# Two attentions mixed by a gate: x loaded with features first, and the gate's row sums taken by PE

## The chip, the cores and the metric

The kernel runs on one core of a Trainium2 chip. The metric is device time in microseconds, smaller is better. The engines are called as in the profile: PE (TensorE, products), PEld (its weight loads), DVE (VectorE), ACT (ScalarE), POOL (GpSimd) and SP (SyncE, which issues most DMAs). A line number such as L279 is a line of the kernel before.

## The reference, cut to what matters

```python
x = A_x                                          # 1 x 2048 x 512, float32
g = sigmoid((x * gate_w).sum(-1, keepdims=True)) # one gate per row of x
a = infini_attention(x, wq, wk, wv, wo, beta)    # 4 segments of 512 rows, causal, with a memory M, z
b = attention(x, wqkv, wo_b)                     # 32 heads of 16, all 2048 rows
return g * a + (1 - g) * b
```

In `infini_attention` each segment's rows also retrieve from the memory of the segments before: `a_mem = (phi(q) @ M) / (phi(q) @ z + 1e-6)`, which is mixed with the causal attention of the segment by `sigmoid(beta)` per head. Everything is float32.

## The kernel before, in words

**Precision.** A product of two float32 operands is made of three products of rounded operands: each operand is split into a rounded part (hi) and the rest (lo), and hi·hi, hi·lo and lo·hi are summed (TERMS). So x, with its 512 features on partitions, is kept twice, as xh (tile XH) and xl (tile XL); weights likewise (ws for q and k, wv for v).

**The x stage** (L642 to L679). x comes as 16 tiles of 128 rows, rows on partitions. SP loads a tile of 256 KB into one of 8 slots of the tile RAW (load_x, L159). PE transposes it in four 128x128 pieces into a PSUM bank (do_x, L168), ACT copies the bank to xh (L171), DVE subtracts to get xl (L172). The gate's row sums are taken on DVE from the same raw tile: dot_gate (L177) multiplies a tile by gate_w, which lies on all 128 partitions (tile gw, 256 KB of DMA), and accumulates along the row into a column of `gate`. After its dot a slot is free, and the loads of tiles 8 to 15 go there. Between these steps stand the eight jobs qk_job(0, "B", 0, w, c): q (w=0) and k (w=1) of the first eight heads of attention B, for each chunk c of 512 rows, 12 products each (L279). A job's result is copied by ACT and DVE into st, one of four buffers, and SP stores it to DRAM in two DMAs (L295). `for c in range(4)`: job w=0, then do_x of the four tiles of the next chunk, two dots and two loads, job w=1, two dots and two loads. POOL loads the weights (L234, L242); the first of them go to VA and to VB[0] (list `flat`), the later ones round the 8 slots of RAW (raw_buf).

**v of attention A** (L686 to L700). 16 jobs v_job("A", tt) of 12 products each (L262), copied by ACT into one of two buffers VS (both lie in VB[0]), stored by SP for two jobs at a time (L269). After job 2 come the split of A's q and k weights and do_gate (sigmoid of the 16 columns of `gate`), after job 3 SP's 12 small loads of beta (L182). POOL loads those weights, and then sends constant rows into the k and q tiles (set_aux, L148). PSUM banks are taken in turn, the one longest unused first (misc; six banks here).

**The 16 blocks** (L722 to L805). For each group of heads g and chunk c: q and k of A, memory out (mem_out, L304), transposes of phi(k) (mem_tr), the memory's output put back by rows (mem_put, L323), and one or more tasks of the list `fill` (v of B, q and k of B's other heads). mem_out writes the retrieved rows to the tile om, mem_put transposes om on PE, scales it back into om, and SP copies om to DRAM (L331). There is one om buffer, so the next block's mem_out waits until that DMA has read it. Near the end of the blocks SP also issues the loads of k for the attention loop (load_kb, L369) and the rows of maxima (m_rows, L484).

**The attention loop** (L905 to L939) runs 32 rounds over both attentions: products of k and q (t_group, L503), exp on ACT (L509), products with v (pv, L525), and ahead of them the products and maxima (s_b, L449 and L451) of the next round. Then come the tail and the output.

The order of each engine's work is the order of the calls in the program; nothing reorders them. A DMA on SP stands behind what was issued before it, and it is issued when what it waits for is done.

Of the kernel before, what the change touches and what calls it, by code (L numbers as in the profile page):

```python
# [7 lines left out]
FT = mybir.dt.float32  # L8
FR = mybir.dt.float32r
BF = mybir.dt.bfloat16  # L10
I32 = mybir.dt.int32
AF = mybir.ActivationFunctionType
OP = mybir.AluOpType
# [5 lines left out]
E = 16  # L19
SEQ = 2048  # L20
DM = 512
C = 512
NC4 = SEQ // C
NT = SEQ // 128
# [6 lines left out]


@with_exitstack
def gated_mix_kernel(ctx, tc, x, wq, wk, wv, wo, beta, wqkv, wob, gate_w, out):
    nc = tc.nc
    xr = x.rearrange("b s d -> (b s) d")
    outr = out.rearrange("b s d -> (b s) d")

    P = ctx.enter_context(tc.tile_pool(name="persist", bufs=1))
    W = ctx.enter_context(tc.tile_pool(name="work", bufs=2))  # L40
# [10 lines left out]
    ident = P.tile([128, 128], FT, name="ident")  # L51
    cmask = P.tile([128, 2, 128], BF, name="cmask")
    crows = P.tile([128, 2, 128], BF, name="crows")
    gate = P.tile([128, NT], FT, name="gate")
# [5 lines left out]
    RAW = P.tile([128, 8, C], FT, name="raw8")  # L60
    PTILE = [RAW[:, 4 * n:4 * n + 4] for n in range(2)]
    xh = [P.tile([128, 2, 4, C], FR, name=f"xh{n}") for n in range(2)]
    XH = [xh[c // 2][:, c % 2] for c in range(NC4)]
    flat = [VA[n].rearrange("p t h e -> p (t h e)")[:, :DM] for n in range(2)]
    vflat = VB[0].rearrange("p t h e -> p (t h e)")
    flat += [vflat[:, n * DM:(n + 1) * DM] for n in range(4)]
    RAWV = flat + [RAW[:, n] for n in range(8)]
    KB = [P.tile([128, 2, SEQ], FR, name="kb0")] + [t.rearrange("p a k t -> p a (k t)") for t in xh]

# [1 line left out]
    X = proj.enter_context(tc.tile_pool(name="proj", bufs=1))  # L71
    XL = [X.tile([128, 4, C], FR, name=f"xl{c}") for c in range(NC4)]
# [15 lines left out]
    def bank(allowed):  # L88
        b = min(allowed, key=lambda a: max([n for n, x in enumerate(lru) if x is a], default=-1))
        lru[:] = [x for x in lru if x is not b] + [b]  # L90
        return b
# [3 lines left out]
    def misc():  # L95
        return bank(mode["misc"])
# [17 lines left out]
    def raw_buf():  # L114
        i = cnt.get("raw", 0)
        cnt["raw"] = i + 1
        return RAWV[i if i < 6 else 6 + (i - 6) % 8]


    def identity():  # L120
        jp = X.tile([128, C], FT, name="phi0").bitcast(I32)[:, :128]
        nc.gpsimd.iota(jp, pattern=[[1, 128]], base=0, channel_multiplier=-1)
        nc.vector.tensor_scalar(ident, jp, 0.0, None, op0=OP.is_equal)

        for j in range(2):
            r = slice(64 * j, 64 * j + 64)
            for n in range(2):
                o = 64.0 * (n - j)
                nc.vector.tensor_scalar(crows[r, n], jp[r], o, None, op0=OP.is_equal)
                nc.vector.tensor_scalar(cmask[r, n], jp[r], o, MASK, op0=OP.is_gt, op1=OP.mult)  # L130
# [18 lines left out]
                                         aux[:, a, None, :].to_broadcast([E, n, 64]))  # L149


    gw = X.tile([128, DM], FT, name="gw")

    def load_gate():
        nc.sync.dma_start(gw, bass.AP(tensor=gate_w.tensor, offset=gate_w.offset, ap=[[0, 128], [1, DM]]))

    XR = {}

    def load_x(tt):  # L159
        XR[tt] = RAW[:, tt % 8]  # L160
        nc.sync.dma_start(XR[tt], xr[tt * 128:(tt + 1) * 128, :])

    def do_x(tt):
        c, tl = divmod(tt, 4)
        xt = XR.pop(tt)
        b = misc().rearrange("p (k t) -> p k t", k=4)
        for k in range(4):
            nc.tensor.transpose(b[:, k, :], xt[:, k * 128:(k + 1) * 128], ident)  # L168
        hi = XH[c][:, :, tl * 128:(tl + 1) * 128]
        lo = XL[c][:, :, tl * 128:(tl + 1) * 128]  # L170
        nc.scalar.activation(hi, b, AF.Copy)  # L171
        nc.vector.tensor_tensor(lo, b, hi, op=OP.subtract)  # L172
        XG[tt] = xt

    XG = {}

    def dot_gate(tt):  # L177
        scr = W.tile([128, DM], BF, name="scr", bufs=1)
        nc.vector.scalar_tensor_tensor(scr, XG.pop(tt), 1.0, gw, op0=OP.mult, op1=OP.mult,
                                       accum_out=gate[:, tt:tt + 1])  # L180

    def load_beta():  # L182
        for g in range(4):
# [13 lines left out]

    def do_gate():
        e = X.tile([128, NT], FT, name="ge")
        nc.scalar.activation(e, gate, AF.Exp, scale=-1.0)  # L200
        nc.vector.tensor_scalar(e, e, 1.0, None, op0=OP.add)
        nc.vector.reciprocal(gate, e)

# [16 lines left out]
    def split(hi, lo, raw):  # L220
        nc.scalar.activation(hi, raw, AF.Copy)
        nc.vector.tensor_tensor(lo, raw, hi, op=OP.subtract)

    def wcols(kd, w):
        if kd == "A":
            return (wq, wk, wv)[w], 0
        return wqkv, w * DM

    WR = {}

    def load_wv(kd, k):
        src, c0 = wcols(kd, 2)
        WR[k] = raw_buf()
        nc.gpsimd.dma_start(WR[k], src[k * 128:(k + 1) * 128, c0:c0 + DM])  # L234

    def split_wv(k):
        split(WV[0][:, k, :], WV[1][:, k, :], WR.pop(k))

    def load_w_raw(kd, g, w):
        src, c0 = wcols(kd, w)  # L240
        raw = raw_buf().rearrange("p (k c) -> p k c", k=4)
        nc.gpsimd.dma_start(raw, src.rearrange("(k p) c -> p k c", p=128)[:, :, c0 + g * 128:c0 + (g + 1) * 128])  # L242
        return raw

    def load_w(kd, g):
        WR[kd, g] = [load_w_raw(kd, g, w) for w in range(2)]

    def split_w(n, kd, g, ws=(0, 1)):
        for w in ws:
            split(WS[n][w][0], WS[n][w][1], WR[kd, g][w])  # L250
# [50 lines left out]
    def mem_state(g, c):  # L301
        return MST[c % 2][g % 2]

    def mem_out(g, c):  # L304
        m = mem_state(g, c)[:, :, :E + 1]
        o = X.tile([128, 4, 8, E], FT, name="om")
        r = X.tile([128, 4, 8], FT, name="recm")
        for n in range(2):
            b = misc()[:, :16 * (E + 1)].rearrange("p (i h e) -> p i h e", i=2, h=8)
            for i in range(2):  # L310
                nc.tensor.matmul(b[:, i], PHI[g, 0, c][:, (2 * n + i) * 128:(2 * n + i + 1) * 128], m,
                                 start=True, stop=True)
            nc.scalar.activation(r[:, 2 * n:2 * n + 2], b[:, :, :, E], AF.Copy)
            nc.scalar.activation(o[:, 2 * n:2 * n + 2].rearrange("p i h e -> p (i h) e"),
                                 b[:, :, :, :E].rearrange("p i h e -> p (i h) e"), AF.Copy)
        nc.vector.tensor_scalar(r, r, 1e-6, None, op0=OP.add)
        nc.vector.reciprocal(r, r)
        nc.vector.tensor_tensor(r, r, gate[:, 4 * c:4 * c + 4, None].to_broadcast([128, 4, 8]), op=OP.mult)
        o3 = o.rearrange("p i h e -> p (i h) e")
        nc.vector.tensor_tensor(o3, o3, r.rearrange("p i h -> p (i h)")[:, :, None].to_broadcast([128, 32, E]), op=OP.mult)  # L320
        PHI[g, "o", c] = o
# [19 lines left out]
    def load_vm(g, c):  # L341
        PHI[g, "v", c] = X.tile([128, 4, 8, E + 1], FT, name="vm", bufs=2)
        v_src(PHI[g, "v", c], "A", g, c)
# [45 lines left out]
    def load_kb(k, c=None):  # L389
        dst = KB[k % 3] if c is None else KB[k % 3][:, :, c * C:(c + 1) * C]  # L390
        load_qk(dst, "B", 1, k % 8, c)
# [247 lines left out]
    def s_tasks(u):  # L639
        return [todo(s_a, u, *t) for t in ST_A] if u < 32 else [todo(s_b, u, *t) for t in ST_B]  # L640

    for tt in range(4):  # L642
        load_x(tt)
    identity()
    load_w("B", 0)
    for tt in range(4, 8):
        load_x(tt)
    load_gate()
    constants()

    for tt in range(3):
        do_x(tt)
    split_w(0, "B", 0, (0,))
    do_x(3)
    split_w(0, "B", 0, (1,))
    def dots(tt):
        for t in (tt, tt + 1):
            dot_gate(t)
            if t + 8 < NT:
                load_x(t + 8)  # L660

    dots(0)
    dots(2)
    for c in range(NC4):
        for w in range(2):
            qk_job(0, "B", 0, w, c)
            if c + 1 < NC4:
                if w == 0:
                    for t in range(4):
                        do_x(4 * c + 4 + t)  # L670
                dots(4 * c + 4 + 2 * w)
            elif w == 0:
                split_wv(3)
        if c == 1:
            for k in range(4):
                load_wv("A", k)
        if c == 2:
            for k in range(3):
                split_wv(k)  # L679
# [6 lines left out]
    for tt in range(NT):  # L686
        v_job("A", tt)
        if tt == 2:
            split_w(0, "A", 0)
            do_gate()  # L690
        if tt == 3:
            load_beta()
        if tt in (7, 9, 11):
            load_wv("B", (tt - 7) // 2)
        if tt == NT - 1:
            load_vm(0, 0)
            load_kb(0)
            load_q(32)
        if ax:
            set_aux(*ax.pop(0))  # L700
# [21 lines left out]
    for blk in range(16):  # L722
        g, c = divmod(blk, 4)
# [9 lines left out]
        n = blk + 1 + (c == 2)  # L733
# [222 lines left out]
    for t in range(4):  # L956
        d = den[:, t * 128:(t + 1) * 128]
        o = o_cols(3, t)[:, 3, 0]
# [36 lines left out]
```

## Time and profile before

| | us |
|---|---|
| median of 3 runs | 1981.27 (1977.9 to 1982.19) |
| span of the profiled execution | 1976.0 |
| x stage: PE busy in the first 44 us | 35.19 |
| of it the transposes (L168) | 10.34 |
| the attention loop, from 350 us to the end | 1626 |

How to read the profile: a row of a group gives line, engine, operation, output<-input, shapes, count, then busy time and mean ns, then the idle time ahead of it and what ended it. A timeline row gives the start and the length in us, engine, line, and in brackets the idle time before it and its releaser. The chain of work that ended last gives the start and the length of each piece. The granted clock is that of PE, 1.00 at full speed. "SPq" is the time in which SP issues a DMA, or waits in doing so.

### The profile page before, as it was taken

How to read it: one execution, taken by the hardware profiler on the slowest of the kernel's cores; microseconds unless marked ns; L12 is line 12 of the kernel's file. 1: busy time of each engine (PE TensorE's matmuls, PEld its weight loads, DVE VectorE, ACT ScalarE, POOL GpSimd, SP SyncE). 2: the span in 40 equal slices, each digit the busy share in tenths (PEclk: the TensorE clock that was granted, in tenths of full speed). 3: DMA queues.
4: the chain of work that ended last, by engine and by line, in shares of the span. 5: the costliest groups of instructions: out<-in, count | busy, mean ns of one | idle time of the engine just before them, and what ended most of it. 6: DMA issues, size and time to landing. Idle time of an engine off the chain costs nothing.

```text
span 1976.0 us, 43643 instructions
## 1 busy us (share of the span) xinstructions
PE 1944.8 (98%) x17517; PEld 945.6 (48%) x17517; DVE 1630.3 (83%) x1825; ACT 1435.7 (73%) x2703; POOL 257.5 (13%) x474
## 2 busy tenths in 40 slices
PE   8999999999999999999999999999999999999999
PEld 6887777434344344444444444444444444444435
DVE  6135665899999999999999999999999999999942
ACT  3233332688888888888888888888888888888884
POOL 2200000011210101111010101010101010101012
PEclk9999999999999999999999999999999999999999
DMA  6766656644443444344445353444344444444111
GB/s 205 172 209 183 191 186 173 152 111 114 97 114 88 103 86 103 86 114 86 114 85 112 86 113 86 114 86 114 86 108 91 96 102 87 102 90 103 48 51 57
DMA packets 162742, 222.49 MB, mean 113 GB/s; under 512 B 39260, under 2 KB 89452, under 8 KB 156780
## 3 DMA queue, kind: packets, MB, share of 16 engines
q1 hardware_dynamic: 159596, 211.70, 44.0%
q0 software_dynamic: 2944, 8.00, 2.1%
q8 instruction: 138, 2.26, 0.5%
q14 instruction: 64, 0.52, 0.1%
HBM read 148.21 MB, written 68.16 MB: 109 GB/s over the span
## 4 chain that ended last, share of the span: by engine, by line
PE 90%; DMA 3%; DVE 2%; ACT 2%; issue 1%; SPq 1%; ACTq 0%; DVEq 0%
PE pvb L525 31%; PE tb L503 17%; PE sbk L449 12%; PE mb L503 8%; PE tb L279 3%; PE tb L591 2%; PE mb L279 2%; PE sbk L427 2%; PE pvb L279 2%; PE tb L262 2%; DVE mxb L451 1%; ACT raw L509 1%; PE mb L591 1%; PE mb L262 1%; PE sbk L431 1%
## 5 line engine op out<-in xcount | busy, mean ns | idle before, releaser
L451 DVE TENSOR_REDUCE mxb<-sbk 128x2 f32<-128x1024 f32 x1024 | 1226.1, 1222 | 36.6 <-PE sbk L449 32.4
L509 ACT ACTIVATE raw<-tb 128x512 f32<-128x512 f32 x1557 | 888.2, 598 | 163.1 <-PE tb L503 90.7
L525 PE MATMUL pvb<-raw,vb 128*17 128x256 f32 (+1 forms) x8072 | 639.4, 388 | 0.0
L509 ACT ACTIVATE raw<-mb 128x512 f32<-128x512 f32 x780 | 466.4, 598 | 76.5 <-PE tb L503 44.8
L503 PE MATMUL tb<-qb,xh 64*128 64x512 f32 x872 | 330.8, 496 | 1.7 <-ACT raw L509 1.7
L525 PEld LDWEIGHTS pvb<-raw,vb 128*17 128x17 f32 x8072 | 134.4, 95 | 341.7 <-issue 336.6
L449 PE MATMUL sbk<-xh,qb 64*128 64x512 f32 x1344 | 283.1, 398 | 2.0 <-DMA xh<-dB 0.8
L503 PE MATMUL mb<-qb,xh 64*128 64x512 f32 x445 | 219.6, 494 | 0.0
L503 PEld LDWEIGHTS tb<-qb,xh 64*128 64x128 f32 x872 | 124.4, 183 | 188.1 <-issue 91.4
L512 POOL TENSOR_SCALAR_AFFINE_SELECT raw<-raw 128x256 f32<-128x256 f32 (+1 forms) x320 | 116.1, 363 | 700.1 <-ACT raw L509 692.3
L503 PE MATMUL tb<-qb,kb 64*128 64x512 f32 x471 | 176.3, 496 | 1.4 <-DMA qb<-mr 0.8
L435 DVE TENSOR_REDUCE mx<-sbk 128x2 f32<-128x768 f32 (+1 forms) x128 | 139.8, 1092 | 43.1 <-PE sbk L431 37.1
L449 PE MATMUL sbk<-kb,qb 64*128 64x512 f32 x704 | 150.6, 406 | 1.2 <-DVE mxb L451 1.1
L449 PEld LDWEIGHTS sbk<-xh,qb 64*128 64x128 f32 x1344 | 137.9, 186 | 7.3 <-DVE mxb L451 3.5
L503 PEld LDWEIGHTS mb<-qb,xh 64*128 64x128 f32 x445 | 81.3, 183 | 86.6 <-issue 48.0
L503 PE MATMUL mb<-qb,kb 64*128 64x512 f32 x233 | 115.4, 495 | 0.7 <-DVE st L289 0.7
L565 POOL TENSOR_TENSOR o<-o,d 128x512 f32<-128x512 f32 x31 | 39.8, 1283 | 562.6 <-DMA d<-rd 281.6
L503 PEld LDWEIGHTS tb<-qb,kb 64*128 64x128 f32 x471 | 66.0, 183 | 98.4 <-issue 52.5
L525 PE MATMUL pvb<-raw,va 128*17 128x256 f32 (+2 forms) x1280 | 94.7, 383 | 5.8 <-ACT pvs L534 5.8
L427 PE MATMUL sbk<-ka,qa 64*128 64x256 f32 (+3 forms) x512 | 86.8, 346 | 1.2 <-ACT raw L509 1.2
L503 PE MATMUL tb<-qa,ka 64*128 64x384 f32 (+3 forms) x340 | 79.2, 372 | 0.0
L449 PEld LDWEIGHTS sbk<-kb,qb 64*128 64x128 f32 x704 | 71.6, 185 | 12.6 <-issue 6.5
(273 smaller groups left out, 1790.7 us busy)
## 6 DMA issues: line engine op xcount, KB each, us to landing
xh<-dB SPq DMA_DIRECT2D x38, 512.0 KB
vb<-vdB SPq DMA_DIRECT2D x16, 1088.0 KB
dB<-st SPq DMA_DIRECT2D x64, 256.0 KB
dA<-st SPq DMA_DIRECT2D x64, 256.0 KB
pd<-pvs SPq DMA_DIRECT2D x64, 256.0 KB
kb<-dB SPq DMA_DIRECT2D x22, 512.0 KB
xh<-dB SPq DMA_DIRECT2D x38, 256.0 KB
qb<-dB SPq DMA_DIRECT2D x64, 128.0 KB
```

The source lines that it names most:

```text
L262: nc.tensor.matmul(b, lhs, WV[wi][:, k, :], start=n == 0, stop=n == 11)
L279: nc.tensor.matmul(b, WS[ws][w][wi][:, k, :], (XH, XL)[xi][c][:, k, :], start=n == 0, stop=n == 11)
L427: nc.tensor.matmul(b[:, j, c0:c0 + n], q_of(u)[r, p, i * 128:(i + 1) * 128], k_of(u, p)[r, :n], start=True, stop=False)
L435: nc.vector.tensor_reduce(m[:, :, p, i], b[:, :, :n], axis=AX.X, op=OP.max)
L449: nc.tensor.matmul(b[:, j], q_of(u)[r, p, i * 128:(i + 1) * 128], k_of(u, p)[r, kc * C:(kc + 1) * C], start=True, stop=True)
L451: nc.vector.tensor_reduce(MXB[u][:, :, p, i, kc], b, axis=AX.X, op=OP.max)
L503: nc.tensor.matmul(bs[j][:, c0:c0 + w], k_of(u, h // 2)[r, 128 * it:128 * it + 128], q_of(u)[r, h // 2, q0:], start=True, stop=True)
L509: nc.scalar.activation(pt, bs[j], AF.Exp, scale=SCALE)
L512: nc.gpsimd.affine_select(out=m, in_=m, pattern=[[1, 128]] if n < 2 else [[0, 2], [1, 128]], compare_op=OP.is_ge, fill=0.0, base=0, channe ...
L525: nc.tensor.matmul(PVB[32 * h:32 * h + E + 1, q0 + lo:q0 + hi], vt[:, it, 4 * q + h, :], pt[:, lo:hi], start=it == 0 and lo == 0, stop=it ...
L565: nc.gpsimd.tensor_tensor(o, o, d, op=OP.mult)
L591: nc.tensor.matmul(b, (AT["oh"], AT["ol"])[oi][:, g, a], (AT["wh"], AT["wl"])[wi][:, g, a], start=n == 0, stop=n == 11)
```

## The change

The host hands x over transposed (512 features by 2048 rows), and the kernel loads it only so: xh and xl are split straight from the loaded chunk, without PE. A chunk is 1 MB; the first is loaded in four quarters. Chunks 0 and 1 lie in the two halves of RAW, chunk 2 in VB[0], chunk 3 in chunk 1's half, so its load waits for the last reader of chunk 1, which is dot_x(1). ACT makes xh; DVE makes xl for features 0 to 255, POOL for the rest.

The gate's sums are now over partitions. dot_x multiplies and adds, on DVE, the four feature blocks of a chunk by a column of gate_w each, into a tile of 128 x 512 that mem_tr, mem_out and qk_job use later (phi0, phi1, om, pk); sum_x adds over the partitions by 16 products on PE with a column of ones. do_gate comes after v_job 3 and not 2. gate_w is loaded as 128 x 4 on ACT's queue; the weights of q for the first jobs are loaded on ACT's queue too. A's v weights now go to RAW, behind chunk 0's readers. om has two buffers.

```diff
-    flat += [vflat[:, n * DM:(n + 1) * DM] for n in range(4)]
...
-        return RAWV[i if i < 6 else 6 + (i - 6) % 8]
+        return RAWV[i if i < 2 else 2 + (i - 2) % 8]
...
-    def do_x(tt):
-        c, tl = divmod(tt, 4)
-        xt = XR.pop(tt)
-        b = misc().rearrange("p (k t) -> p k t", k=4)
-        for k in range(4):
-            nc.tensor.transpose(b[:, k, :], xt[:, k * 128:(k + 1) * 128], ident)
...
-        nc.scalar.activation(hi, b, AF.Copy)
-        nc.vector.tensor_tensor(lo, b, hi, op=OP.subtract)
...
+    XS = [RAW[:, 4 * (c % 2):4 * (c % 2) + 4] for c in range(NC4)]
+    XS[2] = vflat[:, :4 * C].rearrange("p (k t) -> p k t", k=4)
+
+    def load_xt(c, ks=slice(0, 4)):
+        nc.sync.dma_start(XS[c][:, ks], xt.rearrange("(k p) t -> p k t", p=128)[:, ks, c * C:(c + 1) * C])
+
+    def split_x(c, ks):
+        nc.scalar.activation(XH[c][:, ks], XS[c][:, ks], AF.Copy)
+        eng = nc.vector if ks.start < 2 else nc.gpsimd
+        eng.tensor_tensor(XL[c][:, ks], XS[c][:, ks], XH[c][:, ks], op=OP.subtract)
...
-    def dot_gate(tt):
-        scr = W.tile([128, DM], BF, name="scr", bufs=1)
-        nc.vector.scalar_tensor_tensor(scr, XG.pop(tt), 1.0, gw, op0=OP.mult, op1=OP.mult,
-                                       accum_out=gate[:, tt:tt + 1])
+    def dot_x(c):
+        n, sh = (("phi0", [128, C]), ("phi1", [128, C]), ("om", [128, 4, 8, E]), ("pk", [128, 4, 128]))[c]
+        t = X.tile(sh, FT, name=n, bufs=1 + (c == 2))
...
+        nc.vector.tensor_scalar(t, XS[c][:, 0], gw[:, 0:1], None, op0=OP.mult)
+        for k in range(1, 4):
+            nc.vector.scalar_tensor_tensor(t, XS[c][:, k], gw[:, k:k + 1], t, op0=OP.mult, op1=OP.add)
+
+    def sum_x():
+        b = misc()[:, :NT]
+        for tt in range(NT):
+            nc.tensor.matmul(b[:, tt:tt + 1], XG[tt // 4][:, tt % 4 * 128:tt % 4 * 128 + 128], one,
+                             start=True, stop=True)
+        return b
...
-        nc.scalar.activation(e, gate, AF.Exp, scale=-1.0)
+        nc.scalar.activation(e, sum_x(), AF.Exp, scale=-1.0)
...
-        o = X.tile([128, 4, 8, E], FT, name="om")
+        o = X.tile([128, 4, 8, E], FT, name="om", bufs=2)
...
+    WR["B", 0] = [load_w_raw("B", 0, w, (nc.scalar, nc.gpsimd)[w]) for w in range(2)]
+    for k in range(4):
+        load_xt(0, slice(k, k + 1))
+    load_gate()
+    for c in range(1, 3):
+        load_xt(c)
...
     for c in range(NC4):
         for w in range(2):
             qk_job(0, "B", 0, w, c)
-            if c + 1 < NC4:
-                if w == 0:
-                    for t in range(4):
-                        do_x(4 * c + 4 + t)
-                dots(4 * c + 4 + 2 * w)
-            elif w == 0:
+            if w:
+                dot_x(c)
+                if c == 1:
+                    load_xt(3)
+            elif c + 1 < NC4:
+                for n in range(2):
+                    split_x(c + 1, slice(2 * n, 2 * n + 2))
+            else:
                 split_wv(3)
```

More of the change, by code (lines that the diff above doesn't have):

```diff
@@ L33, in gated_mix_kernel @@
 @with_exitstack
-def gated_mix_kernel(ctx, tc, x, wq, wk, wv, wo, beta, wqkv, wob, gate_w, out):
+def gated_mix_kernel(ctx, tc, xt, wq, wk, wv, wo, beta, wqkv, wob, gate_w, out):
     nc = tc.nc
-    xr = x.rearrange("b s d -> (b s) d")
     outr = out.rearrange("b s d -> (b s) d")
@@ L149, in set_aux @@
                                          aux[:, a, None, :].to_broadcast([E, n, 64]))
-    gw = X.tile([128, DM], FT, name="gw")
+    gw = X.tile([128, 4], FT, name="gw")
+    one = X.tile([128, 1], FT, name="one")
+    nc.vector.memset(one, 1.0)
     def load_gate():
[L155 to L161, printed above, removed]
@@ L163, in do_x @@
-    def do_x(tt):
-        c, tl = divmod(tt, 4)
-        xt = XR.pop(tt)
-        b = misc().rearrange("p (k t) -> p k t", k=4)
-        for k in range(4):
[L168 to L171, printed above, removed]
-        nc.vector.tensor_tensor(lo, b, hi, op=OP.subtract)
-        XG[tt] = xt
-    XG = {}
-    def dot_gate(tt):
-        scr = W.tile([128, DM], BF, name="scr", bufs=1)
-        nc.vector.scalar_tensor_tensor(scr, XG.pop(tt), 1.0, gw, op0=OP.mult, op1=OP.mult,
-                                       accum_out=gate[:, tt:tt + 1])
+        nc.scalar.dma_start(gw, bass.AP(tensor=gate_w.tensor, offset=gate_w.offset, ap=[[1, 128], [128, 4]]))
@@ new lines, in gated_mix_kernel @@
+    XG = {}
+    def dot_x(c):
+        n, sh = (("phi0", [128, C]), ("phi1", [128, C]), ("om", [128, 4, 8, E]), ("pk", [128, 4, 128]))[c]
+        t = X.tile(sh, FT, name=n, bufs=1 + (c == 2))
+        XG[c] = t = t if c < 2 else t.rearrange("p i h e -> p (i h e)" if c == 2 else "p i r -> p (i r)")
+        nc.vector.tensor_scalar(t, XS[c][:, 0], gw[:, 0:1], None, op0=OP.mult)
+        for k in range(1, 4):
+            nc.vector.scalar_tensor_tensor(t, XS[c][:, k], gw[:, k:k + 1], t, op0=OP.mult, op1=OP.add)
@@ L237, in split_wv, with load_w_raw @@
         split(WV[0][:, k, :], WV[1][:, k, :], WR.pop(k))
-    def load_w_raw(kd, g, w):
+    def load_w_raw(kd, g, w, eng=None):
         src, c0 = wcols(kd, w)
         raw = raw_buf().rearrange("p (k c) -> p k c", k=4)
-        nc.gpsimd.dma_start(raw, src.rearrange("(k p) c -> p k c", p=128)[:, :, c0 + g * 128:c0 + (g + 1) * 128])
+        (eng or nc.gpsimd).dma_start(raw, src.rearrange("(k p) c -> p k c", p=128)[:, :, c0 + g * 128:c0 + (g + 1) * 128])
         return raw
@@ L640, in s_tasks @@
         return [todo(s_a, u, *t) for t in ST_A] if u < 32 else [todo(s_b, u, *t) for t in ST_B]
-    for tt in range(4):
-        load_x(tt)
+    WR["B", 0] = [load_w_raw("B", 0, w, (nc.scalar, nc.gpsimd)[w]) for w in range(2)]
[4 more added lines that the diff above has]
+        load_xt(c)
     identity()
[L645 to L648, printed above, removed]
+    split_w(0, "B", 0, (0,))
+    for k in range(4):
+        split_x(0, slice(k, k + 1))
+    split_w(0, "B", 0, (1,))
     constants()
[L651 to L663, printed above, removed]
     for c in range(NC4):
@@ L689, in gated_mix_kernel @@
             split_w(0, "A", 0)
+        if tt == 3:
             do_gate()
@@ L983 @@
     for name in _INS:
-        a = _np.ascontiguousarray(inputs[name])
+        a = _np.ascontiguousarray(inputs[name][0].T if name == "A_x" else inputs[name])
         arrays[f"in_{name}_dram"] = a
```

## The prediction

> **What bounds the kernel now.** I read the page first: shares, slices, costliest groups. Then the stretches, which say how much of the span the edits can reach at all, then the chain that ended last inside the first stretch.
>
> ```profile
> span 1976.0 us, 43643 instructions
> PE 1944.8 (98%) x17517; PEld 945.6 (48%) x17517; DVE 1630.3 (83%) x1825; ACT 1435.7 (73%) x2703; POOL 257.5 (13%) x474
> PE   8999999999999999999999999999999999999999
> DVE  6135665899999999999999999999999999999942
> L451 DVE TENSOR_REDUCE mxb<-sbk 128x2 f32<-128x1024 f32 x1024 | 1226.1, 1222 | 36.6 <-PE sbk L449 32.4
> ...
> L525 PE MATMUL pvb<-raw,vb 128*17 128x256 f32 (+1 forms) x8072 | 639.4, 388 | 0.0
> ```
>
> PE is busy 98% of the span; from slice 8 on DVE is at 9 as well. Those slices are the attention loop, which the diff does not touch: it can only start earlier or later.
>
> ```profile
> 0.00:44.00 44.00, 35.19 (x160) 28.46 (x161) 30.45 (x72) 17.08 (x30) 6.54 (x20) 0.96 0.65 211
> 44.00:92.00 48.00, 48.00 (x209) 38.99 (x208) 5.21 (x9) 11.83 (x23) 17.08 (x31) 1.00 0.73 164
> 92.00:350.00 258.00, 252.18 (x1225) 192.08 (x1224) 144.69 (x231) 83.34 (x183) 12.69 (x20) 0.99 0.63 188
> 350.00:1976.00 1626.00, 1609.47 (x15930) 686.10 (x15926) 1449.96 (x1515) 1323.43 (x2469) 221.21 (x403) 1.00 0.43 96
> ```
>
> Columns: stretch, length, busy us of PE, PEld, DVE, ACT, POOL, granted clock, DMA share, GB/s. The x stage is the first 44 us (PE 35.19 busy, about 9 idle). In the next 48 us (v_job of A) PE has no gap: what starts it earlier is gained, what is added to it is paid. The chain inside the first stretch ends so:
>
> ```profile
> 25.24 7.77 DMA raw<-in_A_x_dram
> ...
> 33.05 0.66 PE tb L168 x4
> 33.71 0.69 PE mb L168 x4
> 34.40 4.31 PE pvb L279 x12
> 38.71 5.57 PE sbk L279 x24
> 44.28 5.56 PE tb L262 x24
> ```
>
> The last x tiles set the end of the stage: a 256 KB load took 7.8 us from issue to use, because SP's queue also carries the stores of st (L295). After the pause a job of 12 products takes 4.31 us, later ones 5.57/2 = 2.79. So the question is when the last quarter of x is there, in both kernels.
>
> **The change part by part.** The sum goes against this execution's span of 1976.0 us; the page gives no other time of it. The median 1981.27 lies 5.3 above, and I carry those 5.3 over unchanged.
>
> *Removed: transposes and row dots.*
>
> ```profile
> 0.00:44.00 44.00, 10.34 (x64) 8.40 (x64) 0.96 0.65 211
> L179 DVE SCALAR_TENSOR_TENSOR scr<-raw,gw 128x512 bf16<-128x512 f32 x16 | 11.0, 688 | 3.1 <-DMA gw<-in_gate_w_dram 2.8
> ```
>
> The first row is line L168 alone: 64 transposes, 10.34 us of PE. They go. Of DVE the 16 dots become 16 operations of the same size (4 in each dot_x), 0.69 each: about nothing. PE's removed time counts only if x comes soon enough, so I walk the new stage with these rows:
>
> ```profile
> 8.55 1.09 PE L168 MATMUL pvb<-ident,raw 128*128 128x128 f32 x4
> 9.68 0.60 ACT L171 ACTIVATE xh<-pvb 128x512 fp32r<-128x512 f32 x1
> L584 ACT ACTIVATE oh<-o 128x1024 fp32r<-128x1024 f32 x12 | 12.7, 1058 | 0.0
> L585 POOL TENSOR_TENSOR ol<-o,oh 128x1024 fp32r<-128x1024 f32 x12 | 28.6, 2380 | 6.6 <-ACT oh L584 6.6
> 17.00:20.00 3.00, 3.00 (x15) 2.42 (x14) 3.00 (x7) 1.03 (x3) 0.00 (x0) 1.00 0.95 307
> 34.00:39.00 5.00, 5.00 (x18) 3.98 (x17) 2.69 (x6) 1.14 (x3) 0.00 (x0) 0.66 0.53 204
> ```
>
> Step 1, chunk 0. It is as many bytes as x tiles 0 to 3, ahead of the rest in SP's queue, as now; tile 3 was transposed at 8.55. So its last quarter is there near 8.5, xh at 9.2 (0.60 on ACT), and xl of quarters 2 and 3, now on POOL (half of 2.38 each), near 11.6. At the slow rate after a pause (4.31 for 12) the first job ends near 13.0. Second job: 15.8.
>
> Step 2, chunks 1 and 2. ACT makes xh in halves of 1.06, POOL the second half of xl in 2.38. ACT gets to chunk 1 only behind the first st copy (13.8), so xh is done at 15.9, POOL at 18.3, and the third job ends near 18.8, the fourth at 21.6. Chunk 2 in the same way: POOL is done at 23.9, the jobs at 24.4 and 27.2.
>
> Step 3, chunk 3, the step that decides. Its buffer is chunk 1's; load_xt(3) stands behind dot_x(1) in SP's queue, and dot_x(1) on DVE behind the fourth job's st: 21.6 + 0.60 + 0.69 + 4 x 0.69 = 25.7. Behind this wait SP holds the stores of the fifth and later jobs, and those hold the four st buffers; they have slack. How long 1 MB takes there the trace does not show. Lower end: the first tile was in use 2.8 us after the first issue (0.81 to 3.58 in the rows below), and 0.75 MB more at 307 GB/s, the rate of the stretch that only loads, is 2.6: 5.4. Upper end: the 7.77 of the tile and 2.6: 10.4. Ahead of it stand the stores of one job (0.5 MB at 204 GB/s, the stretch that only stores: 2.6), and beside it load_wv(A), 1 MB on POOL's queue, which used to run in the first 15 us and now waits for dot_x(0) and for POOL's subtracts. I take 7: landed at 32.7.
>
> Step 4. xh at 33.8; PE has waited since 27.2. After a pause come 4.31 and 2.79, and I add 0.9 because this pause, 6.6 us, is longer than the one in the chain: v_job starts near 41.8, before 44.3. **Gain 2.5.** Of the 10.34 removed most goes into this wait.
>
> ```profile
> 0.81 4.22 SPq L161 DMA_DIRECT2D raw<-in_A_x_dram  x8
> 3.58 1.94 PE L168 MATMUL tb<-ident,raw 128*128 128x128 f32 x8 [3.58 <-DMA raw<-in_A_x_dram]
> 106.62 1.10 PE L311 MATMUL tb<-mst,phi 128*128 128x136 f32 x8
> 121.24 0.63 PE L311 MATMUL sbk<-mst,phi 128*128 128x136 f32 x4
> L311 PE MATMUL tb<-mst,phi x48: 277/278/383, 106.6 to 334.7; 128*128 128x136 f32 x48
> ```
>
> *Added: sum_x on PE.* 16 products of a 128x128 f32 operand by one column, between v_job 3 and 4. f32 products are two instructions each here (L311: 4 products, x8), so 32 pairs of weight load and product. The nearest row is L311, which loads as much weight: 8 take 1.10, 4 take 0.63, so (1.10 - 0.63)/4 = 0.117 each, 3.8 us. With one column instead of 136 it could be less: L525, with small weights, runs at 639.4/8072 = 0.079, 2.5 us. Were nothing overlapped: 32 x 0.278 = 8.9. I take 3.8; PE has no gap there, so nothing hides it. **Loss 3.8.**
>
> [...]
>
> *Does the rest of the stage follow?*
>
> ```profile
> 45.05 0.76 POOL L242 DMA_DIRECT2D raw<-in_A_wq_dram  x1 [0.30 <-issue]
> 82.26 0.60 ACT L267 ACTIVATE vb<-mb 128x512 f32<-128x512 f32 x1 [13.91 <-DMA vdA<-vb]
> 82.95 2.09 PE L262 MATMUL mb<-wv,xh 128*128 128x512 f32 x8
> ```
>
> v_job's copies wait for the stores of v, up to 13.9 us, and PE starts the next job in bank mb 0.1 us after that bank's copy ends: no slack is left. That chain begins with POOL's load_w at 45.05, which will wait for dot_x(3): 41.8 + 0.60 + 0.69 + 0.69, about 43.8, 1.3 earlier than now. So the chain comes 1.2 us less early than v_job's start, PE behind sum_x 3.8 less: PE is the later one whatever step 4 gives, and no new stall comes of it. Were sum_x nearly free, the chain would take 1.2 of the gain.
>
> *Two om buffers.*
>
> ```profile
> 126.06 0.39 ACT L314 ACTIVATE om<-pvb 128x256 f32<-128x256 f32 x1 [3.45 <-DMA om<-om]
> 128.19 0.66 PE mb L327 x4
> 341.86 0.38 ACT L314 ACTIVATE om<-tb 128x256 f32<-128x256 f32 x1 [6.65 <-DMA om<-om]
> 342.30 3.78 PE L279 MATMUL tb<-xh,wv 128*128 128x512 f32 x8 [3.00 <-ACT om L314]
> 344.02 2.58 SPq L484 DMA_DIRECT2D qb<-mr  x2
> 349.33 0.50 PE L503 MATMUL tb<-qb,kb 64*128 64x512 f32 x2 [0.83 <-DMA qb<-mr]
> ```
>
> The wait of 6.65 on ACT goes, with it 3.0 us of idle PE and the slow clock behind it (3.78 for what takes 2.1): 5 us and more of PE. But what is late next is written in the last two rows: the attention loop's first product waits for qb<-mr, which SP issues at 344.02 behind loads of kb and stores, none of which waits for om's copy. PE would only stand there longer, and start colder. At 128 a few tenths of PE go. I count 0.3 gained, bounds 5 gained and 2 lost.
>
> Shorter gw load, no scr, the memset of one: no engine of the path, nothing.
>
> Sum: -2.5 + 3.8 - 0.3 = +1.0. **1981.27 + 1.0 = 1982.3 us**, span 1977.0.
>
> **The rivals.**
>
> *A, x never waited for.* If chunk 3 lands by 28 (asked for sooner, or in 5.4 from 22), the eight jobs run through and v_job starts near 33: gain 11.3, less 3.8 and with the 0.3: 1973.5. For: DMA share is only 0.65. Against: step 3's chain through dot_x(1).
>
> *B, the om wait was worth its 5 us.* 1982.3 - 4.7 = 1977.6, just inside 0.2%; with a front a little better, 1976. Against: SP's issue at 344.02.
>
> *C, slower: the wait on chunk 3 takes the place of the transposes and more.* At 10.4 us it lands at 36.1, v_job starts at 45.2: +0.9 + 3.8 - 0.3 = +4.4, 1985.7. It decides from a landing at 35.7 on. For: the tile with 7.77 is the only row of such a load behind stores.
>
> *D, the products don't overlap:* 8.9 instead of 3.8, 1987.4. Against: L311's 0.117.
>
> [...]
>
> *F, the edit does not do what it says:* the stage was bound by SP's queue, v_job starts at 44.3 as before: +3.8 - 0.3, 1984.8.
>
> **How the numbers follow.** My forecast has 0.34, A 0.16, B 0.10, C 0.14, D 0.08, E 0.08, F 0.10. About 0.2% (4 us) is what a measurement of this kernel can tell from no change: 1977.3 to 1985.2. Faster: A and most of B, 0.24. Slower: C, D and an edge of E, 0.24. Same: 0.52. The predicted time is that of the forecast, 1982. The range 1974 to 1988 holds all but half of A and the far ends of C and D.
>
> **What would show it.** Step 3 is right if PE stands idle before the seventh job of qk_job for 4 to 8 us, released by ACT's xh, with DMA raw<-in_A_x behind it; wrong if PE runs through (A) or v_job starts after 44.3 (C, F). The products: 32 pairs in about 3.8 us near 53. The om wait is gone from ACT, and the attention loop's first product (t_group) still waits for qb<-mr, longer than 0.83. Any change of more than 2 us in the length of the attention loop would mean that I have missed an effect altogether.

## The result, and the profile after

| | median, us | against before, same chip (95% interval) |
|---|---|---|
| before | 1981.65 (7 runs) | |
| after | 1988.28 (1984.5 to 1991.73, 7 runs) | 1.0033 (1.0017 to 1.0049) |

The change makes the kernel slower, by 6.6 us in the medians (3.4 to 9.7 by the interval); 1.0 slower had been forecast. The profiled execution of after took 1985.57, with a span of 1983.8. Lines after L200 are three higher than before: L282 is qk_job's product (was L279), L265 v_job's, L181 sum_x's, L506 t_group's.

The same stretches as for before; columns: stretch, length, busy us of PE, PEld, DVE, ACT, POOL, granted clock, DMA share, GB/s.

```profile
0.00:44.00 44.00, 26.28 (x89) 19.46 (x90) 23.31 (x37) 16.40 (x24) 16.20 (x23) 0.88 0.62 202
44.00:92.00 48.00, 47.76 (x217) 39.09 (x216) 10.62 (x17) 10.40 (x19) 17.37 (x32) 0.96 0.69 153
92.00:350.00 258.00, 255.50 (x1251) 195.56 (x1249) 144.42 (x230) 84.41 (x185) 12.66 (x20) 1.00 0.62 187
350.00:1983.00 1633.00, 1612.03 (x15935) 687.86 (x15932) 1450.03 (x1516) 1324.53 (x2471) 221.30 (x403) 1.00 0.42 97
```

The transposes are gone: PE is busy 26.28 us of the x stage instead of 35.19. But the stage is not shorter. PE's idle time in it grew from 9 to 18 us, its clock fell from 0.96 to 0.88, and in the next stretch, where PE has hardly a gap (47.76 busy of 48.00), the clock is 0.96 instead of 1.00. The timeline of after shows where (start, length, engine, line, in brackets the idle time before it and what ended it):

```profile
22.18 3.15 POOL L166 TENSOR_TENSOR xl<-vb,xh 128x1024 fp32r<-128x1024 f32 x1 [3.47 <-ACT xh L164]
...
23.64 1.99 DVE L174 TENSOR_SCALAR phi<-raw,gw 128x512 f32<-128x512 f32 x1
...
25.27 2.19 POOL L237 DMA_DIRECT2D raw<-in_A_wv_dram  x4
...
28.05 0.38 SPq L161 DMA_DIRECT2D raw<-in_A_x_dram  x1
...
37.53 2.00 ACT L164 ACTIVATE xh<-raw 128x1024 fp32r<-128x1024 f32 x2 [10.77 <-DMA raw<-in_A_x_dram]
...
38.63 3.56 PE L282 MATMUL tb<-xh,ws 128*128 128x512 f32 x8 [9.72 <-ACT xh L164]
...
45.75 1.79 PE L265 MATMUL mb<-wv,xh 128*128 128x512 f32 x7
...
47.79 0.50 PE L265 MATMUL mb<-wv,xh 128*128 128x512 f32 x1 [0.24 <-DVE wv L225]
...
57.40 1.84 PE L181 MATMUL tb<-one,phi 128*128 128x1 f32 x16
...
60.89 2.69 PE L265 MATMUL tb<-wv,xh 128*128 128x512 f32 x8
63.38 1.91 PE L265 MATMUL tb<-wv,xl 128*128 128x512 f32 x4
65.08 2.25 PE L265 MATMUL mb<-wv,xh 128*128 128x512 f32 x8
```

The same places in the timeline of before, the start of v_job and the last transposes of om:

```profile
44.12 2.02 PE L262 MATMUL tb<-wv,xh 128*128 128x512 f32 x8
...
347.59 0.92 PE L327 MATMUL mb<-ident,om 128*128 128x128 f32 x4
```

Three things are to be read here. **Chunk 3** is issued at 28.05 and in use at 37.53, 9.5 us later; PE stands 9.72 us for it, nearly as long as all the transposes had taken, and v_job starts at 45.75 instead of 44.12, 1.6 later. Four more executions with this front (experiments 2, 3, 5 and 6) have the chunk in use 9.0 to 10.0 us after its issue and v_job at 45.4 to 46.7. The front of before varies more: v_job starts at 44.98 in experiment 11 and at 41.89 in experiment 12, where no half clock follows the wait for x. So the 1.6 is that of one pair of executions, and it can be 0.5 to 4.8. **sum_x** takes 57.40 to 60.89, 3.5 us. **Behind sum_x** the next v_job takes 60.89 to 65.08, 4.2 us, where a job takes 2.8. That is the clock:

```profile
57.00:62.20 5.20, 5.20 (x41) 4.89 (x40) 1.81 (x4) 1.93 (x4) 2.65 (x5) 1.00 0.95 121
62.20:65.60 3.40, 3.40 (x10) 2.62 (x9) 0.00 (x0) 0.00 (x0) 0.53 (x1) 0.50 0.97 174
```

PE is busy throughout, and its clock is half for 3.4 us. At the end of the blocks the second om buffer took its wait away, and another one stood behind it:

```profile
349.62 0.60 PE L330 MATMUL tb<-ident,om 128*128 128x128 f32 x4
...
350.33 2.21 SPq L487 DMA_DIRECT2D qb<-mr  x2
...
355.77 0.79 PE L506 MATMUL tb<-qb,kb 64*128 64x512 f32 x1 [5.55 <-DMA qb<-mr]
```

Before, PE came to this transpose at 347.59, after it had waited 3.00 us for om; now it comes without a wait, and stands 5.55 us at the attention loop's first product, which starts at 355.77 instead of 349.33: 6.4 later.

A caution on the traces: one execution of each kernel was profiled. After's lies 2.7 us under its median; before's took about 1977.8 (its span and the 1.8 that after has beyond its own), 3.8 under. A second profile of before (experiment 11) has a span of 1982.5, 1.3 under that of after. Traces are therefore compared by places, and prices are taken from the ratios where these are fine enough.

### The profile page after: what moved, and what is told of

It is laid out like the page before. It is cut to its first block, busy times and chain, and to the rows that moved or that the text cites. A ratio compares the mean times of both kernels' runs of the same rounds, so it can differ in the third digit from the quotient of the medians.

```text
span 1983.8 us, 43513 instructions
## 1 busy us (share of the span) xinstructions
PE 1941.6 (98%) x17485; PEld 942.0 (47%) x17485; DVE 1628.4 (82%) x1799; ACT 1435.7 (72%) x2697; POOL 267.5 (13%) x478
## 4 chain that ended last, share of the span: by engine, by line
PE 92%; ACT 2%; DVE 2%; DMA 1%; issue 1%; SPq 0%; ACTq 0%; DVEq 0%
PE pvb L528 32%; PE tb L506 17%; PE sbk L452 13%; PE mb L506 8%; PE tb L282 4%; PE tb L594 2%; PE mb L282 2%; PE sbk L430 2%; PE pvb L282 1%; PE sbk L265 1%; ACT raw L512 1%; PE tb L265 1%; PE mb L594 1%; DVE mxb L454 1%; PE sbk L434 1%
## 5 line engine op out<-in xcount | busy, mean ns | idle before, releaser
L506 PE MATMUL tb<-qb,xh 64*128 64x512 f32 x872 | 331.0, 494 | 2.0 <-ACT raw L512 2.0
L506 PE MATMUL mb<-qb,xh 64*128 64x512 f32 x445 | 220.5, 496 | 0.0
L506 PEld LDWEIGHTS tb<-qb,xh 64*128 64x128 f32 x872 | 124.1, 183 | 180.0 <-issue 89.9
L506 PE MATMUL tb<-qb,kb 64*128 64x512 f32 x470 | 179.4, 496 | 6.9 <-DMA qb<-mr 5.5
L506 PEld LDWEIGHTS mb<-qb,xh 64*128 64x128 f32 x445 | 81.3, 183 | 95.4 <-issue 50.8
L506 PEld LDWEIGHTS tb<-qb,kb 64*128 64x128 f32 x470 | 68.1, 183 | 105.3 <-issue 52.0
L506 PE MATMUL mb<-qb,kb 64*128 64x512 f32 x234 | 116.4, 497 | 0.0
L289 ACT ACTIVATE st<-tb 128x512 fp32r<-128x512 f32 x33 | 19.7, 598 | 88.2 <-DVE phi L288 46.0
L506 PE MATMUL tb<-qa,ka 64*128 64x512 f32 (+3 forms) x339 | 79.5, 372 | 0.0
```

The lines of the kernel that those rows point to most:

```text
L506: nc.tensor.matmul(bs[j][:, c0:c0 + w], k_of(u, h // 2)[r, 128 * it:128 * it + 128], q_of(u)[r, h // 2, q0:], start=True, stop=True)
```

## The experiments

Each ratio is against runs of the kernel before on the same chip; after stands at 1.0033.

**1. Chunk 3 in a place of its own** (two quarters in a new tile, two where the first raw weights were), loaded ahead of all stores.

```diff
+    XS[3] = X.tile([128, 2, C], FT, name="xs3")
+    HALF = {(3, 2): flat[0][:, None], (3, 3): flat[1][:, None]}
...
     for c in range(1, 3):
         load_xt(c)
+    load_xt(3, slice(0, 2))
...
     split_w(0, "B", 0, (1,))
+    for k in range(2, 4):
+        load_xt(3, slice(k, k + 1))
...
-                if c == 1:
-                    load_xt(3)
```

> The changed kernel with a place of its own for chunk 3 of x (two quarters in a new tile, two in the places of the first raw weights), so that its load no longer waits for dot_x(1). Theory (chunk 3's late load holds the front): PE no longer stands before the seventh job of qk_job; v_job starts between 35 and 40 us instead of 45.75, and 6 to 9 us of it arrive at the end: about 1981 against 1988.3. Rival 1 (GpSimd and VectorE disturbing one another sets the front): v_job still starts after 43, 1986 to 1988. Rival 2 (the stores of v and their buffers take it back): v_job starts early, but PE gets new waits before 92 us and less than 3 us are left: 1986.

Measured: 1977.52, ratio 0.9982 (0.9970 to 0.9994): faster than before, and 0.51% below after (10 us; 6 to 14 by the two intervals). The timeline of this kernel:

```profile
27.98 2.02 PE L288 MATMUL tb<-xh,ws 128*128 128x512 f32 x8
...
34.23 1.96 PE L271 MATMUL mb<-wv,xh 128*128 128x512 f32 x7
...
46.38 1.84 PE L187 MATMUL tb<-one,phi 128*128 128x1 f32 x16
...
50.21 3.76 PE L271 MATMUL tb<-wv,xh 128*128 128x512 f32 x8
```

PE passes from chunk 2 to chunk 3 (27.98) without a wait, and v_job starts at 34.23: 11.5 us earlier than in after. The late load of chunk 3 held the front. Of the 11.5 us some is paid back behind sum_x, where the half clock is now 6.8 us long:

```profile
46.30:49.50 3.20, 3.20 (x31) 3.16 (x29) 0.00 (x0) 0.60 (x1) 1.11 (x3) 1.00 0.92 217
49.50:56.30 6.80, 6.80 (x19) 5.48 (x19) 0.43 (x2) 0.18 (x1) 3.63 (x7) 0.50 0.95 216
```

**2. Without sum_x's products.**

```diff
-        nc.scalar.activation(e, sum_x(), AF.Exp, scale=-1.0)
+        nc.scalar.activation(e, XG[0][:, :NT], AF.Exp, scale=-1.0)
```

> The changed kernel without the 16 products of sum_x (32 pairs of weight load and product); the sigmoid is taken of 16 columns of dot_x(0) instead, so the gate is not that of the reference. Theory (the block of small products and the half clock behind it cost 5.1 us of PE that nothing hides): the half clock at 62 to 65 us is gone and the end comes 5 us earlier, 1983.3. Rival (the stores of v are as late, and the copies of v_job would hold PE anyway): PE waits for the copies of v_job instead, 1 to 2 us gained, 1986.5 or more.

Measured: 1984.2, ratio 1.0014 (1.0004 to 1.0025), 0.19% (3.8 us) below after; the half clock at 62 us is gone, and PE comes to the last transposes of om 3.15 us earlier (346.47 against 349.62). The products cost 3.8 by the medians, and the two intervals together leave anything from 0 to 7.6; after's trace, where block and half clock can be read, says 5.1. The rival (the stores of v) fell: PE has no new wait before 92 us.

**3. One om buffer.**

```diff
-        o = X.tile([128, 4, 8, E], FT, name="om", bufs=2)
+        o = X.tile([128, 4, 8, E], FT, name="om")
...
-        t = X.tile(sh, FT, name=n, bufs=1 + (c == 2))
+        t = X.tile(sh, FT, name=n)
```

> The changed kernel with one om buffer. Theory (the second buffer moves only a wait, since the attention loop's first product waits for qb<-mr): ACT's wait of 6 to 7 us before om near 345 comes back, the end is 0 to 1 us later: 1988.3 to 1989.3. Rival (the second buffer is worth the 3 us of idle PE and the slow products behind it): 4 to 5 us later, 1993.

Measured: 1992.51 (6 runs, 1989.03 to 1998.87), ratio 1.0064 (1.0043 to 1.0086), 0.31% above after (6 us; 1 to 11 by the two intervals). The theory was too low, and the rival's size is the nearer one, though not by its mechanism. PE waits at two places for what one buffer holds up. The first is at 135 us:

```profile
133.12 0.38 ACT L317 ACTIVATE om<-tb 128x256 f32<-128x256 f32 x1 [5.34 <-DMA om<-om]
...
135.25 0.66 PE L330 MATMUL sbk<-ident,om 128*128 128x128 f32 x4 [2.19 <-DVE om L323]
```

The second is the one that the theory spoke of: the loop's first product comes at 357.43 instead of 355.77, since qb<-mr itself is issued later (352.01 instead of 350.33). The half clock behind it is 10.2 us long instead of 6.8, and there is one more of 3.4 us at 1916; of the two traces of before, both with one buffer, one has a half clock near there and one has none (experiment 11). Against after this kernel falls back by 2.4 us between 65 and 176 us and by 1.9 between 332 us and the loop's start. So by the traces the second buffer is worth about 4 us, 2 at each place; what the longer half clocks add is not in that, and the ratio's 6 would hold both.

The same kernel has sum_x's block at 56.87 to 60.36, 3.5 us as in after, and the same stretch as above reads

```profile
62.20:65.60 3.40, 3.40 (x17) 2.76 (x16) 0.00 (x0) 0.00 (x0) 1.06 (x2) 1.00 0.90 151
```

so the half clock is not there in each execution.

**4. xl on VectorE alone.**

```diff
-        eng = nc.vector if ks.start < 2 else nc.gpsimd
-        eng.tensor_tensor(XL[c][:, ks], XS[c][:, ks], XH[c][:, ks], op=OP.subtract)
+        nc.vector.tensor_tensor(XL[c][:, ks], XS[c][:, ks], XH[c][:, ks], op=OP.subtract)
```

> The changed kernel with all of xl made by VectorE, none by GpSimd. Theory (chunk 3's load behind dot_x(1) is the cause, GpSimd only adds to it): dot_x's operations go back from 0.9 to 2.0 us to about 0.7, VectorE gets 1.4 us of subtracts more for each chunk, so load_xt(3) is issued within 2 us of 28.05 and v_job starts within 2 us of 45.75: 1986.5 to 1990. Rival (GpSimd's subtracts beside dot_x's operations are what made the front late): load_xt(3) is issued near 25.5, v_job starts near 42, 1984.

Measured: 1989.79, ratio 1.0048 (1.0030 to 1.0065): no gain on after.

```profile
23.93 0.48 DVE L173 TENSOR_SCALAR phi<-raw,gw 128x512 f32<-128x512 f32 x1
...
26.80 0.37 SPq L161 DMA_DIRECT2D raw<-in_A_x_dram  x1
...
37.92 2.00 ACT L164 ACTIVATE xh<-raw 128x1024 fp32r<-128x1024 f32 x2 [12.93 <-DMA raw<-in_A_x_dram]
```

The operation that took 1.99 us beside GpSimd's subtract takes 0.48 without it, so the two do disturb one another, and the load is issued 1.25 us earlier. It is in use no earlier (37.92 against 37.53). GpSimd isn't the cause of the late chunk.

**5 and 6. The copies qb<-mr and qa<-mr of the first round on ACT's queue**, with two om buffers and with one.

```diff
-                nc.sync.dma_start(q_of(u).bitcast(FT)[48 + a:128:64], mr[r:r + 16])
+                (nc.sync if k else nc.scalar).dma_start(q_of(u).bitcast(FT)[48 + a:128:64], mr[r:r + 16])
```

> The changed kernel with the first qb<-mr and qa<-mr copies issued by ACT's queue instead of behind the stores in SP's. Theory (the second om buffer left PE standing at the attention loop's first product, 5.55 us, because these copies were issued at 350.33 though mr was ready at 342.2): they are issued before 345, the wait goes and with it the half clock behind it: 5 to 8 us gained, 1980 to 1983. Rival (the loads and stores ahead of them in SP's queue are needed too, another wait takes over): under 2 us gained, 1986.5 or more.

> The same copies on ACT's queue, but with one om buffer. Theory (the second buffer is worth its 3 us of idle PE only where qb<-mr does not come later): 3 to 5 us slower than with two buffers. Rival (the second buffer's worth is the same whatever qb<-mr does): slower by the same 4 us as one buffer was behind SP's queue; rival 2 (it is worth nothing): within 1 us of two buffers.

Measured: 1984.01, ratio 1.0007 (0.9996 to 1.0018), 0.26% below after (5 us; 1 to 9 by the two intervals), with two; 1992.88, 1.0047 (1.0032 to 1.0061) with one, 0.4% (8 us) above that. With two om buffers:

```profile
342.47 1.69 ACTq L487 DMA_DIRECT2D qb<-mr  x2
...
349.90 0.60 PE L330 MATMUL tb<-ident,om 128*128 128x128 f32 x4
...
350.43 0.50 PE L506 MATMUL tb<-qb,kb 64*128 64x512 f32 x1
```

mr was ready 8 us before SP got round to it. On a queue with nothing ahead the copies are issued at 342.47, and PE runs on without a wait. With one buffer in that arrangement the om wait is back in its old size, and here nothing later covers it:

```profile
358.20 0.38 ACT L317 ACTIVATE om<-tb 128x256 f32<-128x256 f32 x1 [5.33 <-DMA om<-om]
...
360.33 0.66 PE L330 MATMUL tb<-ident,om 128*128 128x128 f32 x4 [2.90 <-DVE om L323]
```

The 8 us are more than the 3 to 5 expected, since PE also stood 1.72 us for om at 139 us, and between 320 and 344 us lost some 4 us more, to a load that came late (PE 2.12 us for xh) and to a half clock (8 products with vm in 2.18 us, where the same took 1.19 at 320).

**7. Own place, and the products in four groups of 4.**

```diff
+    def sum_x(c):
+        b = misc()[:, :4]
+        for i in range(4):
+            nc.tensor.matmul(b[:, i:i + 1], XG[c][:, i * 128:i * 128 + 128], one, start=True, stop=True)
+        nc.scalar.activation(ge[:, 4 * c:4 * c + 4], b, AF.Exp, scale=-1.0)
...
             qk_job(0, "B", 0, w, c)
+            if w == 0 and c > 1:
+                sum_x(c - 2)
...
+        if tt == 1:
+            sum_x(2)
```

> Chunk 3 in its own place, and the 16 products in four groups of 4: those of chunks 0 and 1 after the fifth and seventh job of qk_job, those of chunk 2 after the second v_job, those of chunk 3 after the fourth. Theory (the block of 32 light pairs makes the clock fall to half behind it, 3.4 or 6.8 us long, 1.5 us of PE for each 3.4): no half clock between 40 and 60 us, 2.5 to 3.5 us less than with the own place alone: near 1974.5. Rival (the clock falls for another reason, the waits of the x stage before it): the half clock stays, within 1 us of 1977.5.

Measured: 1972.9, ratio 0.9951 (0.9938 to 0.9963), 0.31% (6 us) below the own place alone, where 2.5 to 3.5 had been expected; by the traces v_job 8 comes 4.1 earlier, and 2 us more come up inside the attention loop, where these runs do not say from what. No half clock up to 92 us:

```profile
0.00:36.00 36.00, 27.96 (x114) 21.34 (x115) 25.55 (x40) 16.55 (x25) 19.28 (x29) 1.00 0.72 240
36.00:48.00 12.00, 11.66 (x55) 9.35 (x54) 7.90 (x12) 4.19 (x10) 6.16 (x12) 1.00 0.95 171
48.00:92.00 44.00, 44.00 (x196) 35.99 (x195) 6.37 (x17) 11.99 (x24) 8.99 (x17) 1.00 0.70 178
```

Same products, same count: of the 4.1 us some 3 are the half clock behind the block, and 0.6 the block itself, which takes 3.83 us in one piece (46.38 to 50.21) and 0.81 for each group of 4.

**8. All three: own place, groups, copies on ACT's queue.**

> Own place for chunk 3, products in four groups, qb<-mr and qa<-mr on ACT's queue, two om buffers. Theory (the three causes lie behind one another on PE and add): 1988.3 less 10.8 (measured for the own place), less 3, less 5 to 8: 1967 to 1970. Rival (with PE so early, the loads of the attention loop, kb and xh from dB, come late and take part of it back): 1971 to 1976.

Measured: 1967.05, ratio 0.9923 (0.9909 to 0.9937): as the theory had it, the causes add. This version beats both kernels, before by 0.77%. From its page:

```profile
span 1964.5 us, 43515 instructions
...
PE 1938.4 (99%) x17485; PEld 940.9 (48%) x17485; DVE 1627.4 (83%) x1799; ACT 1435.6 (73%) x2701; POOL 267.5 (14%) x479
```

**9. Own place, but the load stays at its old point in SP's queue.**

```diff
                 dot_x(c)
                 if c == 1:
-                    load_xt(3)
+                    for ks in ((0, 2), (2, 3), (3, 4)):
+                        load_xt(3, slice(*ks))
```

(with the places of experiment 1.)

> Chunk 3 in its own place, but its load stands in SP's queue where it stands in the changed kernel, behind the stores of the fourth job: only the wait for dot_x(1) is taken away. Theory 1 (the load is late because dot_x(1) holds its issue until 28.05): issued near 24, in use 9 us later, near 33.5, v_job near 42. Theory 2 (it is late because it shares eight DMA engines with the stores of st, which keep them busy without a gap from 17 to 38 us at 170 to 200 KB a us): issued near 24, but in use no earlier than 36, v_job within 1.5 us of 45.75; only a load ahead of all stores gets through early.

Measured: 1988.85, ratio 1.0035 (1.0025 to 1.0046): no gain on after.

```profile
25.16 1.42 SPq L167 DMA_DIRECT2D xs<-in_A_x_dram  x1
...
35.55 1.06 ACT L170 ACTIVATE xh<-xs 128x1024 fp32r<-128x1024 f32 x1 [8.93 <-DMA xs<-in_A_x_dram]
```

Issued 2.9 us earlier, in use 2.0 earlier: 10.4 us after its issue. This lies between the theories, nearer to the second. At v_job's start 0.9 us of it are left (44.82 against 45.75), where experiment 1, ahead of the stores and of wv's load, gained 11.5. The wait for dot_x(1), which the change put there, is the small part; the place in the line is the large one.

**10. wv's load behind the last chunk's split.**

```diff
-        if c == 1:
-            for k in range(4):
-                load_wv("A", k)
...
+    for k in range(4):
+        load_wv("A", k)
+    for k in range(4):
+        split_wv(k)
     for vs in VS:
```

> The changed kernel with the load of wv behind the last chunk's split, so that its 1 MB no longer moves beside chunk 3 (it is late itself then, and v_job later still; the time is not the point). Theory 1 (wv's load, 0.8 MB between 29 and 33 us, took its share from chunk 3): chunk 3 in use near 34.5 instead of 37.5. Theory 2 (the stores are what it shares with): 36.5 to 38.

Measured in one execution (1991.85; wv itself comes late):

```profile
27.87 0.37 SPq L161 DMA_DIRECT2D raw<-in_A_x_dram  x1
...
34.75 2.00 ACT L164 ACTIVATE xh<-raw 128x1024 fp32r<-128x1024 f32 x2 [8.17 <-DMA raw<-in_A_x_dram]
```

and the stretch from 28 to 38 us

```profile
28.00:38.00 10.00, 2.87 (x9) 1.74 (x8) 2.36 (x4) 2.49 (x3) 1.17 (x1) 0.67 0.56 179
```

Without wv beside it the chunk is in use 6.9 us after its issue, 2.8 sooner than in after. In after the same ten microseconds read

```profile
28.00:38.00 10.00, 0.91 (x4) 0.39 (x3) 0.58 (x1) 0.47 (x1) 0.00 (x0) 0.67 0.81 273
...
17.00:28.00 11.00, 10.29 (x45) 8.06 (x44) 10.32 (x13) 4.13 (x6) 6.99 (x6) 1.00 0.53 171
```

that is 2.7 MB instead of 1.8. Theory 1 holds for 2.6 us of the 9.5, as far as one execution can tell; the other 0.2 is the earlier issue.

**11. The kernel before once more.**

> The kernel before, unchanged, for a second profile. If the first profile was one of the shorter executions (its time of 1977.9 lies 3.7 under the median), the second has one or two more stretches of half clock of 3.4 us, 1.5 us of PE each, and a span of 1978 to 1981; if not, the span is within 1 of 1976.0.

One execution, 1984.26, span 1982.5, of the same code whose first profile had 1976.0. It came 4.0 us later to the loop, after 0.9 more in the x stage, a longer wait for om (PE 1.98 us, where the first profile had 0.30) and a late load of xh; and near the end it has 6.8 us of half clock that the first had not:

```profile
130.65 0.66 PE L327 MATMUL mb<-ident,om 128*128 128x128 f32 x4 [1.98 <-DVE om L320]
```

```profile
1908.60:1915.40 6.80, 6.80 (x32) 4.52 (x33) 5.38 (x12) 1.09 (x2) 0.90 (x1) 0.50 0.14 41
```

**12. The kernel before with two om buffers and the copies on ACT's queue** (the second buffer that experiment 3 takes away, and the edit of experiment 5).

> The kernel before with two edits only: two om buffers, and the first qb<-mr and qa<-mr copies on ACT's queue. Theory (the om wait of 6.65 on ACT costs PE 3.0 us and a slow stretch behind it, and it is to be had once qb<-mr does not come later): 4 to 7 us under the kernel before, 1975 to 1978 where that has 1981.5. Rival (before, PE stood there only 0.83 us for qb<-mr, so that these copies were no matter, and the stores behind om are as late as ever): 0 to 2 us.

Measured: 1976.99, ratio 0.9980 (0.9969 to 0.9991), 4 us faster: the lower end of the theory. So the second buffer, with the copies behind it moved, is a gain apart from the rest of the change; the shares of the two edits were not told apart here.

## Why the prediction was wrong, point by point

- **Step 3 failed**: chunk 3 "landed at 32.7" was forecast, and it was in use at 37.53. The issue was forecast for 25.7 and came at 28.05; half of that is GpSimd's subtract beside dot_x (1.25 us in experiment 4), the rest a fourth job that was 0.8 later and three operations of dot_x at 0.78 us instead of 0.69. The load was put at 7 us and took 9.5. The 7 is right for a load that has only the stores beside it (6.9 in experiment 10); wv's 1 MB was named in the text as lying beside it and was given no price: 2.6 us. I also priced only "the stores of one job" ahead of it. From 17 to 28 us the DMA share is 0.53 at 171 GB/s without a break: the stores of four jobs drained until the moment of issue, so an earlier issue would have helped little (experiments 4 and 9). SP's queue, which holds the stores, took 50.8% of the time of the 16 DMA engines in these 11 us, as much as eight of them fully busy; which engines a store uses no run shows.
- **Step 4** followed from that: v_job was forecast for 41.8 and started at 45.75. Its own 0.9 us for the longer pause was the author's estimate, which no run shows: the job behind the pause took 4.34 us (38.63 to 42.97), where before took 4.31. The term of -2.5 became +1.6, and +2.2 with the wait on wv's lo part. Steps 1 and 2 held within 1.7 us (the sixth job ended at 28.9, forecast 27.2).
- **sum_x was mis-sized** by what comes behind it. The block itself took 3.5 us (forecast 3.8), 0.109 for a pair where 0.117 had been read from L311. The half clock behind it had no term in the sum at all; it added 1.6 in after's trace and 3 in experiment 1.
- **Two om buffers**: the mechanism was right, since qb<-mr did take the wait's place (5.55 us), and experiments 5 and 6 show the worth that it covers. The 0.3 was too small: experiment 3 says about 4 us, within the bounds of +5 and -2. Half of it is the wait near 130 us, which I had put at "a few tenths" from an execution in which it was short (0.30; 2.19 and 1.98 in experiments 3 and 11).
- **No new stall in the chain of v's stores**: right (experiment 2).
- **The rivals**: C is what happened, the wait on chunk 3 takes the transposes' place and more. Its point of decision, a landing at 35.7, was passed at 37.5. Its price of 1985.7 lacked the clock. A would have needed the load ahead of the stores, as experiment 1 has it; B needed the copies moved; D fell. F's number fell (44.3), but its ground, that SP's queue binds the stage, is what experiments 1 and 9 show of the changed kernel. E was the chance that GpSimd's subtract and dot_x hold one another up. They do: beside the subtract dot_x's first operation took 1.99 us instead of the 0.48 of experiment 4, and the subtract 3.15, where that of the last chunk took 2.47 (39.61 to 42.08). But without it the last chunk was in use no earlier (37.92 in experiment 4), so E's price is not shown.
- **The sum by places**: front +2.2 instead of -2.5, sum_x +5.1 instead of +3.8, om -0.6 (against that short wait), all together 6.7 where after's trace stands 7.8 behind the first trace of before. The 1.1 left lies at the start of the attention loop (after, columns as above, granted clock 0.50):

```profile
352.30:359.10 6.80, 3.33 (x10) 2.29 (x11) 2.06 (x2) 1.08 (x2) 0.00 (x0) 0.50 0.48 152
```

Behind the wait for qb<-mr the half clock lasts to 359.1, and the loop's first pieces, up to the second group of products of xh and wv, take 8.4 us (355.77 to 364.17) where before took 6.9 (349.33 to 356.24) at a granted clock of 1.00. From there on the loop is as long as before; its whole length grew by 1.4 us, less than the 2 that the prediction had named as a sign of something missed. These places are those of one trace of each kernel. Against the second trace of before (experiment 11) after stands only 1.3 behind, since that execution of before is later at v_job, om and a load of xh and has a half clock near its end. So the 6.6 of the medians can't be shared out to the last microsecond; the ratios of experiments 1, 2, 3 and 5, with their intervals, say what each part is worth.
- **The carry** of 5.3 us from span to median was no fault: for after it is 4.5.

## What to carry to other kernels

A load that waits for a buffer gets in line behind whatever was stored meanwhile: price it by the bytes ahead of it and beside it, and put loads that decide ahead of the stores (v_job starts 11.5 us earlier so in experiment 1, and 0.9 in experiment 9, where the load stays behind them). Work that PE does in tiny products costs twice here, by its own time (3.5 us) and by the clock behind it (1.6 us in after, 3 in experiment 1), so it goes between large products and not in one block. A wait taken away is worth its full size only when the next late thing, here two small copies at the end of a long queue, is moved too.

## What the runs showed of the hardware that was not expected

Behind the block of sum_x the clock can be half, though PE counts as busy in the profile all the while (in after 5.20 of 5.20 us with the block, 3.40 of 3.40 behind it). Behind the block in one piece the clock was 0.50 for 3.4 us in after (62.20 to 65.60) and for 6.8 us in experiment 1 (49.50 to 56.30), and in experiment 3 it stayed at 1.00 (62.20 to 65.60), with a block as long as after's, 3.5 us. In groups of four (0.81 us each) it did not fall: experiment 7 has 1.00 up to 92 us. The other stretches of half clock in the first traces of the two kernels are as long or a multiple: 3.4 us (from 34.2) and 6.8 (from 341.4) in before, 10.2 (from 31.5) and 6.8 (from 352.3) in after.

That the pairs of a weight load and a one-column product bring the half clock is inferred from these four traces; what decides whether it comes, and for how long, they do not show. In them the block costs 0, 1.6 or 3 us beyond its own time, and this may be one source of the scatter between executions.
